# Causal attention and a gated product on one core: Strassen's seven block products for half of the first two batches' first two matrices

## The chip, the cores and the metric

The kernel runs on one core of one Trainium2 chip. The metric is device time in microseconds of one execution, as the median of timed runs; smaller is better. The engines are TensorE (PE, with its weight loads shown apart as PEld), VectorE (DVE), ScalarE (ACT), GpSimd (POOL) and SyncE (SP), whose queue issues every transfer of this kernel.

## The reference, cut to what matters

Causal attention over 4 batches, 12 heads, 448 positions and a head size of 64; its output, put together as 1792 tokens of 768 features, goes through a gated product with d_ff = 1536. The weights arrive as 64-bit floats, everything else as 32-bit floats.

```python
scores = np.where(mask, -1e9, q @ k.T / 8)
attn = exp(scores - max) / (sum + 1e-9)
x = (attn @ v)                      # (1792, 768), heads side by side
out = ((x @ w_a) * (x @ w_b)) @ w_out
```

## The kernel before, in words

**Numbers.** TensorE is fed with 32-bit values split into a rounded part and a rest (x_hi and x_lo, w_hi and w_lo, g_hi and g_lo). A product of one 128x128 weight tile with 448 columns is three matmuls: hi by hi, hi by lo, lo by hi (products, L631 to L639). They are called products below. A 64-bit weight unit of 128x768 is made into 32-bit floats by five DVE instructions and one ACT instruction (convert_unit, L323 to L352), written back to memory as w_keep, and split (split, L360) by one ACT copy and one DVE subtraction.

**Stages.** First comes the attention of batches 0 and 1, by pairs of heads, twelve pairs. Then stage one, the gated product of batches 0 and 1: for each of 12 slices f of d_ff a unit of w_a and one of w_b, and 12 units of w_out, six after f = 5 and six after f = 11. Each of these 36 units is 36 products: 2 batches by 6 slices of 128 rows of the weights, times 3. The attention of batches 2 and 3 runs beside stage one, twelve pairs more; its result goes to memory (x_keep). Then stage two, the gated product of batches 2 and 3, which goes by Strassen throughout: (w_a, w_b) by (batch 2, batch 3) is a 2x2 block product over the lower and upper half of the features, so seven block products of 9 matmuls, 63 in all, stand for the 72 of two units (seven, L712). Its sums of x blocks are made at the end of stage one (take_first, take_second, L590 to L613) from x_keep, and the sums of weight blocks by prepare_all (L681).

**Attention per pair.** PE computes scores into banks; DVE adds the mask and takes the maximum (L448, seven instructions); ACT takes the exponential and the row sum (L454, seven), then divides (L467, seven, in batches 2 and 3); PE transposes (L490), ACT copies the transposed pieces (pt), PE multiplies by v (L529).

**Order.** Nothing is issued as written. Each step is recorded with an engine, a cost and what it reads and writes (Plan.op), and Plan.order lays them out by a list schedule; the index in which steps are recorded sets their priority. uses (L863) records stage one and two and yields after each three products of stage one; attend (L912) records a pair's steps at fixed yields, a new pair every AT[1] = 30 yields, that is two and a half units. convert_next is two units ahead and split_next one unit ahead of the products that use them.

Of the kernel before, what the change touches and what calls it, by code (L numbers as in the profile page):

```python
# [9 lines left out]
F32 = mybir.dt.float32  # L10
# [35 lines left out]
LEAD = (2, 1)  # L46
# [184 lines left out]
def causal_attention_then_gated_product(  # L231
# [15 lines left out]
    def sb(tag, n, shape, dt=F32):  # L247
        return plan.ring(tag, n, lambda i: sbuf.tile(shape, dt, tag=f"{tag}{i}", name=f"{tag}{i}"))
# [71 lines left out]
    def load_kept(u):  # L320
        w_32.append(load_32(u))

    def convert_unit():  # L323
# [17 lines left out]
        plan.op("act", 840, lambda: nc.scalar.activation(  # L341
            e.t, e.t, AF.Copy, bias=-896.0 * 2**23, scale=8.0), [e], [e])
        plan.op("dve", 900, lambda: nc.vector.scalar_tensor_tensor(  # L343
            out=r(), in0=m.t, scalar=2.0**32, in1=low(), op0=ALU.mult, op1=ALU.add), [m, t], [m])
        plan.op("dve", 900, lambda: nc.vector.scalar_tensor_tensor(  # L345
            out=e.t, in0=high(), scalar=0x80000000, in1=e.t,
            op0=ALU.bitwise_and, op1=ALU.bitwise_or), [t, e], [e])
        plan.op("dve", 900, lambda: nc.vector.scalar_tensor_tensor(
            out=wt.t, in0=r(), scalar=2.0**-52, in1=e.t.bitcast(F32),
            op0=ALU.mult, op1=ALU.mult), [m, e], [wt])  # L350
        load(P * UW * 4, lambda: w_keep[u], lambda: wt.t, [wt], [("keep", u)])
        w_32.append(wt)  # L352

    def half():
        h = plan.ring("w", 6, None)
# [221 lines left out]

    raw_x, spare = {}, []

    def both(o, a, b, op, reads, writes):  # L580
        two_input("dve", S, o, a, b, op, reads, writes)

# [26 lines left out]
    for r in range(2):  # L609
        for h in range(2):  # L610
            for f in range(h * HF, (h + 1) * HF):
                order += [("a", f), ("b", f)] if r == 0 else [("s", f)]
            if r == 1:  # L613
                order += [("oo", NP // 2 * h + j) for j in range(NP // 2)]
            else:
                order += [("o", 2 * e + h) for e in range(ET)]
    place = {"a": lambda n: 2 * n, "b": lambda n: 2 * n + 1, "o": lambda n: NA + n}
    in_turn = [place[kind](n) if kind in place else None for kind, n in order]
    xs, a_sb = {}, {}

    def x_parts():
# [16 lines left out]

        plan.op("pe", 3 * 200, mm, [(w, 0), (w, 1), *keys], [ps])  # L639

    to_load = iter(in_turn[:NU])

    def load_next():
        u = next(to_load, None)
        if u is not None:
            load_words(u)

    turned, parted = [0], [0]

    def convert_next():  # L650
        n = turned[0]
        turned[0] += 1
        if n < NU:
            plan.soonest = HOLD[0] + HOLD[1] * n if n <= LEAD[0] else 0.0
            convert_unit()
            plan.soonest = 0.0
            load_next()
        elif n < len(order):
            kind, f = order[n]
            if n == NU:  # L660
                units = []
                for h in range(2):
                    units += [(place["a"](i), place["b"](i), False) for i in range(h * HF, (h + 1) * HF)]
                    units += [(place["o"](4 * j + h), place["o"](4 * j + 2 + h), True) for j in range(NP // 2)]
                weights.extend([load_32(u) for u in units[0][:2]])
                to_prepare[0] = prepare_all(units)

    def split_next():
        n = parted[0]
        parted[0] += 1  # L670
        if n < len(order):
            kind, f = order[n]
            if kind not in ("s", "oo"):
                split_unit()
            elif kind == "s" and f == 0:
# [5 lines left out]
    def prepare_all(units):  # L681

        for n, (_, _, late) in enumerate(units):
            a, b = weights.pop(0), weights.pop(0)
            for i in range(7):
                if i in (0, 4):
                    if n + 1 < len(units):
                        weights.append(load_32(units[n + 1][i // 4]))
                if i == 0:
# [22 lines left out]
    def seven(f, n):  # L712

        bank_a, bank_b, bank_c = (bank("m", 3) for _ in range(3))

# [7 lines left out]
                   (bank_c, "T1", True), (bank_b, "T4", False), (bank_c, "B22", False))  # L723
        for i, (ps, name, first) in enumerate(plan_of):
            next(to_prepare[0], None)
            w = ready.pop(0)
            for k in range(3):
                (hi, hi_key), (lo, lo_key) = (part[k] for part in block[name])
# [2 lines left out]
                s1 = mid()  # L731
                copy("act", S, lambda: s1.t, lambda: bank_a.t[:, :S], [bank_a], [s1], True)
            elif i == 1:
                u2 = sb("acc", 2, [P, S])
                added(u2, bank_b, s1)
            elif i == 2:
                c11 = mid()
                copy("act", S, lambda: c11.t, lambda: bank_a.t[:, :S], [bank_a], [c11], True)
            elif i == 3:
                u3 = sb("acc", 2, [P, S])  # L740
                added(u3, bank_b, s1)
            elif i == 4:
                c22 = mid()
# [6 lines left out]
            else:  # L750
                c12 = mid()
                added(c12, bank_c, u2)
                if f % HF < 3:
# [108 lines left out]

    def uses():  # L863

        for n, (kind, f) in enumerate(order):
            first = n // NU * 2
            convert_next()
            if n == NU - 5:
                make_rooms()
                take_first(0)  # L870
            elif n == NU - 4:
                take_first(1)
            elif n == NU - 3:
                more_rooms()
                take_second(0)
                take_first(2)
            elif n == NU - 2:
                take_second(1)
            elif n == NU - 1:
                take_second(2)  # L880
            if kind == "s":
                if order[n + 1][0] != "o":
                    split_next()
                seven(f, n)
                yield
                continue
            if kind == "oo":
# [153 lines left out]
```

## Time and profile before

| | us |
|---|---|
| median of three timed runs | 636.47 (635.89 to 636.66) |
| the profiled execution's own time | 637.46 |
| its span | 635.4 |
| PE busy | 625.8 (98%) |
| PEld busy | 555.5 (87%) |
| DVE busy | 511.6 (81%) |
| ACT busy | 367.4 (58%) |
| POOL busy | 46.9 (7%) |

The first products stand at 61.5 us, stage two begins at 403.9 us. TensorE's granted clock is full speed (1.00, the 2.4 GHz level) in every slice. A row of the windows view gives, for one stretch, each engine's busy time with the number of its instructions, then the granted clock, the share of the 16 transfer engines and GB/s. A row of the timeline is start, length, engine, line, operation, output and inputs; the length of a DVE or ACT instruction covers a tail that overlaps the next one, so that the cost of one in a dense run is the distance of two starts.

### The profile page before, as it was taken

How to read it: one execution, taken by the hardware profiler on the slowest of the kernel's cores; microseconds unless marked ns; L12 is line 12 of the kernel's file. 1: busy time of each engine (PE TensorE's matmuls, PEld its weight loads, DVE VectorE, ACT ScalarE, POOL GpSimd, SP SyncE). 2: the span in 40 equal slices, each digit the busy share in tenths (PEclk: the TensorE clock that was granted, in tenths of full speed). 3: DMA queues.
4: the chain of work that ended last, by engine and by line, in shares of the span. 5: the costliest groups of instructions: out<-in, count | busy, mean ns of one | idle time of the engine just before them, and what ended most of it. 6: DMA issues, size and time to landing. Idle time of an engine off the chain costs nothing.

```text
span 635.4 us, 11232 instructions
## 1 busy us (share of the span) xinstructions
PE 625.8 (98%) x4034; PEld 555.5 (87%) x4034; DVE 511.6 (81%) x1143; ACT 367.4 (58%) x874; POOL 46.9 (7%) x104
## 2 busy tenths in 40 slices
PE   9999999999999999999999999999999999999997
PEld 6666779899899899899889888999999999999986
DVE  6789988989777576598597597588899768889994
ACT  6989548578478468568567553244555444445430
POOL 3756320000000000000000000000000000000000
PEclk9999999999999999999999999999999999999999
DMA  8636535755828646435542266321212632222622
GB/s 277 222 117 207 171 141 195 246 175 203 296 93 273 221 179 228 169 127 181 183 153 78 90 202 202 108 75 50 76 51 68 194 113 58 67 58 87 219 97 88
DMA packets 41719, 95.89 MB, mean 151 GB/s; under 512 B 4800, under 2 KB 27840, under 8 KB 41664
## 3 DMA queue, kind: packets, MB, share of 16 engines
q1 hardware_dynamic: 41664, 95.18, 45.0%
q8 instruction: 32, 0.52, 0.3%
q14 instruction: 23, 0.19, 0.1%
HBM read 67.24 MB, written 27.92 MB: 150 GB/s over the span
## 4 chain that ended last, share of the span: by engine, by line
PE 87%; DVE 8%; DMA 2%; ACT 1%; issue 0%; POOL 0%; SPq 0%; POOLq 0%; DVEq 0%
PE m L634 61%; PE t L634 7%; PE t L490 5%; PE s L634 3%; PE s L439 3%; PE pv L634 2%; PE t L439 2%; PE pv L510 1%; PE pv L529 1%; PE m L529 1%; DVE early L448 1%; DVE p L448 1%; DVE pt L293 1%; ACT early L454 1%; DVE x_lo L301 1%; DMA acc<-o_keep 1%
## 5 line engine op out<-in xcount | busy, mean ns | idle before, releaser
L634 PE MATMUL m<-x_hi,w_hi 128*128 128x448 f32 x432 | 160.5, 372 | 0.0
L634 PE MATMUL m<-x_hi,w_lo 128*128 128x448 f32 x432 | 156.4, 362 | 0.0
L634 PE MATMUL m<-x_lo,w_hi 128*128 128x448 f32 x432 | 156.1, 361 | 0.0
L634 PEld LDWEIGHTS m<-x_hi,w_lo 128*128 128x128 f32 x432 | 81.0, 188 | 6.2
L634 PEld LDWEIGHTS m<-x_hi,w_hi 128*128 128x128 f32 x432 | 81.2, 188 | 5.4 <-issue 0.2
L634 PEld LDWEIGHTS m<-x_lo,w_hi 128*128 128x128 f32 x432 | 81.1, 188 | 4.7
L454 ACT ACTIVATE p<-p,st 128x448 f32<-128x448 f32 (+6 forms) x126 | 62.5, 498 | 32.6 <-DVE st L448 32.1
L301 DVE TENSOR_TENSOR w_lo<-w,w_hi 128x384 fp32r<-128x384 f32 (+1 forms) x90 | 64.6, 719 | 13.1 <-ACT w_hi L285 12.8
L285 ACT ACTIVATE w_hi<-w 128x384 fp32r<-128x384 f32 (+1 forms) x90 | 58.2, 648 | 27.4 <-PE m L634 12.5
L285 ACT ACTIVATE w_hi<-w_e_s 128x384 fp32r<-128x384 f32 x72 | 37.3, 522 | 52.4 <-PE m L634 30.1
L285 ACT ACTIVATE mid<-m 128x448 f32<-128x448 f32 x60 | 32.6, 544 | 52.3 <-PE m L634 52.2
L634 PE MATMUL m<-g_hi,w_hi 128*128 128x448 f32 x144 | 53.4, 371 | 1.3 <-DVE mid L301 1.2
L634 PE MATMUL m<-g_hi,w_lo 128*128 128x448 f32 x144 | 52.1, 362 | 0.0
L634 PE MATMUL m<-g_lo,w_hi 128*128 128x448 f32 x144 | 52.1, 362 | 0.0
L301 DVE TENSOR_TENSOR w_lo<-w_e_s,w_hi 128x384 fp32r<-128x384 f32 x72 | 39.7, 552 | 11.4 <-ACT w_hi L285 10.3
L285 ACT ACTIVATE pt<-t 128x512 f32<-128x512 f32 x72 | 40.7, 593 | 9.4 <-PE t L490 9.3
L301 DVE TENSOR_TENSOR mid<-m,mid 128x448 f32<-128x448 f32 x36 | 22.4, 621 | 27.1 <-PE m L634 20.2
L345 DVE SCALAR_TENSOR_TENSOR w_e<-w,w_e 128x768 uint32<-128x768 uint32 x36 | 34.5, 961 | 7.5 <-ACT w_e L341 7.4
L285 ACT ACTIVATE g_hi<-mid 128x448 fp32r<-128x448 f32 x42 | 24.2, 575 | 24.7 <-DVE mid L301 24.6
L341 ACT ACTIVATE w_e<-w_e 128x768 uint32<-128x768 uint32 x36 | 30.2, 845 | 13.3 <-DVE w_e L336 12.9
L467 ACT ACTIVATE p<-p,st 128x64 f32<-128x64 f32 (+6 forms) x84 | 34.9, 497 | 1.0 <-DVE st L463 1.0
L343 DVE SCALAR_TENSOR_TENSOR w_m<-w_m,w 128x768 f32<-128x768 uint32 x36 | 34.4, 954 | 0.4
(153 smaller groups left out, 1305.4 us busy)
## 6 DMA issues: line engine op xcount, KB each, us to landing
w<-w SPq DMA_DIRECT2D x36, 768.0 KB, 4.6
w_keep<-w SPq DMA_DIRECT2D x36, 384.0 KB, 3.3
w<-w_keep SPq DMA_DIRECT2D x36, 384.0 KB, 3.1
raw<-qT SPq DMA_DIRECT2D x24, 224.0 KB, 3.9
raw<-kT SPq DMA_DIRECT2D x24, 224.0 KB, 4.2
o_keep<-mid SPq DMA_DIRECT2D x24, 224.0 KB, 2.0
v<-v SPq DMA_DIRECT2D x24, 192.0 KB, 3.3
x_keep<-acc SPq DMA_DIRECT2D x12, 224.0 KB, 2.1
```

The lines of the kernel that those rows point to most:

```text
L285: return nc.scalar.activation(o(), i(), AF.Copy)
L301: plan.op(engine, ns, lambda: e.tensor_tensor(out=o(), in0=a(), in1=b(), op=op), reads, writes)
L341: plan.op("act", 840, lambda: nc.scalar.activation(e.t, e.t, AF.Copy, bias=-896.0 * 2**23, scale=8.0), [e], [e])
L343: plan.op("dve", 900, lambda: nc.vector.scalar_tensor_tensor(out=r(), in0=m.t, scalar=2.0**32, in1=low(), op0=ALU.mult, op1=ALU.add), [m, ...
L345: plan.op("dve", 900, lambda: nc.vector.scalar_tensor_tensor(out=e.t, in0=high(), scalar=0x80000000, in1=e.t, op0=ALU.bitwise_and, op1=ALU ...
L439: x = nc.tensor.matmul(at[r][0].t[to * D:(to + 1) * D, at[r][1]], q[:, r * D:(r + 1) * D], k[:, 0:D * (r + 1)], start=True, stop=True)
L448: return nc.vector.tensor_tensor_reduce(out=view(r), in0=at[r][0].t[:, at[r][1]], in1=mask[:, S - n:], scale=-0.125, scalar=3.0e38, op0=AL ...
L454: return nc.scalar.activation(view(r), view(r), AF.Exp, bias=st.t[:, nm, r:r + 1], scale=-1.0, accum_out=st.t[:, sm, r:r + 1],)
L467: return nc.scalar.activation(view(r), view(r), AF.Copy, scale=st.t[:, rc, r:r + 1])
L490: x = nc.tensor.matmul(t.t[:, P * i:P * (i + 1)], p.t[:, at:at + P], swapped if r in CROSSED else ident, is_transpose=True, start=True, st ...
L529: r = nc.tensor.matmul((ps, more)[row].t[j * D:(j + 1) * D, D * k:S], vt.t[rows, c, j, :], parts[n].t[rows, j, o:o + NR - k, :].rearrange( ...
L634: r = nc.tensor.matmul(ps.t[:, :S], a[:, i, :], x(), start=first and n == 0, stop=last and n == 2, skip_group_check=part)
```

## The change

In stage one the slices f = 6 to 11 of w_a and w_b (the second half of d_ff) go by the seven block products too, with batches 0 and 1 as the two columns of blocks. Units f = 0 to 5 and all units of w_out stay as they were. For this:

- the twelve weight units of f = 6 to 11 are converted earlier, beside the units 3 to 14 (EXTRA), go to memory, and are read back as 32-bit floats when prepare_all makes their sums and splits;
- the sums of x blocks of batches 0 and 1 are made by the new function take, at units 15 to 17 (TAKES), in rooms that other tiles leave (first_rooms);
- the attention of batches 2 and 3 starts a pair every 12 yields, one unit, where it was 30;
- the costs that the planner assumes for a conversion are lowered (840 to 735, 900 to 869).

```diff
+F0 = 6
-AT = (2, 30)
+AT = (2, 12)
+EXTRA = (0, 0, 0, 1, 1, 1, 1, 1, 1, 1, 1, 1, 1, 1, 1)
+TAKES = (15, 16, 17)
...
+    def first_rooms():
+        (x_hi, x_lo), (y_hi, y_lo) = xs[0], xs[1]
+        for name, hi, lo, at in (("B11", x_hi, x_lo, 0), ("B21", x_hi, x_lo, 3), ("T1", y_hi, y_lo, 0), ("B22", y_hi, y_lo, 3)):
+            block[name] = [[((lambda x=x, k=at + k: x.t[:, k, :]), (x, at + k)) for k in range(3)] for x in (hi, lo)]
...
+    def take(k):
+        rooms = [sb("pt", 3, [P, 1024]) for _ in range(2)]
+        b11, b12, b21, b22 = (((lambda t=t, i=i: t.t[:, i * S:(i + 1) * S]), (t, i)) for t in rooms for i in range(2))
+        for (o, key), b, kk in ((b11, 0, k), (b12, 1, k), (b22, 1, k + 3), (b21, 0, k + 3)):
+            hi, lo = xs[b]
+            both(o, lambda hi=hi, kk=kk: hi.t[:, kk, :].bitcast(F32), lambda lo=lo, kk=kk: lo.t[:, kk, :].bitcast(F32), ALU.add,
+                 [(hi, kk), (lo, kk)], [key])
...
+        less(b11, b12, b11)
+        split_block("T1", k, *b11)
+        less(b12, b22, b12)
+        split_block("T3", k, *b12)
+        less(b22, b22, b11)
+        split_block("T2", k, *b22)
+        less(b21, b21, b22)
+        split_block("T4", k, *b21)
...
-                order += [("a", f), ("b", f)] if r == 0 else [("s", f)]
+                order += [("a", f, r), ("b", f, r)] if r == 0 and f < F0 else [("s", f, r)]
...
+    besides = [place[kind](f) for f in range(F0, FT) for kind in "ab"]
...
+    def convert_one(besides=False):
+        convert_unit(besides)
+        load_next()
...
                     if n + 1 < len(units):
                         weights.append(load_32(units[n + 1][i // 4]))
+                    elif r == 0:
+                        convert_one()
                 if i == 0:
-                    s12, s34 = (plan.ring("w_e", 2, lambda j: sbuf.tile([P, UW], F32, tag=f"w_e{j}", name=f"w_e_s{j}"))
+                    tag, count, width = (("pt", 3, 1024), ("w_e", 2, UW))[r]
+                    s12, s34 = (plan.ring(tag, count, lambda j: sbuf.tile([P, width], F32, tag=f"{tag}{j}", name=f"{tag}_s{j}"))
...
+                if r == 0:
+                    both(lambda: c12.t, lambda: c12.t, lambda: c22.t, ALU.mult, [c22], [c12])
+                    part_g(3, f, lambda: c12.t, c12)
+                elif f % HF < 3:
...
+            if n in TAKES:
+                if n == TAKES[0]:
+                    first_rooms()
+                take(TAKES.index(n))
...
             split_next()
+            for _ in range(EXTRA[n] if n < len(EXTRA) else 0):
+                convert_one(True)
```

**On PE, the products of f = 6** (m is a bank, x_hi, x_lo the parts of one batch's x, t a bank of transposes, raw_x a block sum kept where q and k lay). Before, with a pair's transposes between the products:

```order
L490 MATMUL t_2945<-swapped,p_70 128x128
L490 MATMUL t_2945<-ident,p_70 128x128
L490 MATMUL t_2945<-swapped,p_70 128x128 x2
L490 MATMUL t_2953<-ident,p_70 128x128
L490 MATMUL t_2953<-swapped,p_70 128x128
L490 MATMUL t_2953<-ident,p_70 128x128 x2
L634 MATMUL m_2830<-x_hi_431,w_hi 128x448
L634 MATMUL m_2830<-x_lo_450,w_hi 128x448
L634 MATMUL m_2830<-x_hi_431,w_lo 128x448
L634 MATMUL m_2967<-x_hi_944,w_hi 128x448
L634 MATMUL m_2967<-x_lo_966,w_hi 128x448
L634 MATMUL m_2967<-x_hi_944,w_lo 128x448
```

After, in the first f that goes by seven block products:

```order
L677 MATMUL m_3565<-raw_x_3369,w_hi 128x448 x2
L677 MATMUL m_3565<-raw_x_3369,w_lo 128x448
L677 MATMUL m_3565<-raw_x_3435,w_hi 128x448 x2
L677 MATMUL m_3565<-raw_x_3435,w_lo 128x448
L677 MATMUL m_3565<-raw_x_3501,w_hi 128x448 x2
L677 MATMUL m_3565<-raw_x_3501,w_lo 128x448
L677 MATMUL m_3618<-x_hi_944,w_hi 128x448
L677 MATMUL m_3618<-x_lo_966,w_hi 128x448
L677 MATMUL m_3618<-x_hi_944,w_lo 128x448
```

The attention's transposes have moved ahead of this place, and the block sum T3 takes the place of a batch's x. Over the whole program PE has 2376 products where it had 2430; every other kind of matmul keeps its count.

**On DVE, between two pairs of the attention of batches 2 and 3** (w_e, w_m and w are the words, the mantissa and the result of a conversion, w_lo the rest of a split). Before:

```order
L301 TENSOR_TENSOR mid_2253<-m_2219,mid_2071 128x448
L301 TENSOR_TENSOR w_lo<-w_1980,w_hi 128x768
L301 TENSOR_TENSOR g_lo<-mid_2253,g_hi 128x448
L348 SCALAR_TENSOR_TENSOR w_2277<-w_m,w_e_2077 128x768
L301 TENSOR_TENSOR w_lo<-w_2063,w_hi 128x768
L301 TENSOR_TENSOR mid_2300<-m_2204,mid_2137 128x448
L348 SCALAR_TENSOR_TENSOR w_2306<-w_m,w_e_2123 128x768
L301 TENSOR_TENSOR g_lo<-mid_2300,g_hi 128x448
L336 TENSOR_SCALAR w_e_2317<-w_2069 128x768
```

After:

```order
L341 TENSOR_SCALAR w_m<-w_1846 128x768
L348 SCALAR_TENSOR_TENSOR w_e_2002<-w_1846,w_e_2002 128x768
L346 SCALAR_TENSOR_TENSOR w_m<-w_m,w_1846 128x768
L465 TENSOR_SCALAR st<-st 128x7
L304 TENSOR_TENSOR acc_2082<-m_2040,acc_2082 128x384
L467 RECIPROCAL st<-st 128x7
L351 SCALAR_TENSOR_TENSOR w_2102<-w_m,w_e_2002 128x768
L339 TENSOR_SCALAR w_e_2111<-w_1924 128x768
L341 TENSOR_SCALAR w_m<-w_1924 128x768
L304 TENSOR_TENSOR w_lo<-w_2016,w_hi 128x768
L346 SCALAR_TENSOR_TENSOR w_m<-w_m,w_1924 128x768
```

Two conversions and one split now stand between two pairs, and a pair follows every unit. The split of a unit stands 12 to 39 products ahead of the unit's first product, from unit 3 to unit 17; before it stood 0 to 72 ahead there.

**On SP, the end of stage one** (x_keep holds the attention of batches 2 and 3, raw takes it back for the block sums, acc and out belong to w_out). Before:

```order
L304 DMA raw_4274<-x_keep_5_122 128x448
L304 DMA x_keep_5_128<-acc_4276 128x448
L304 DMA w_4297<-w_keep_82 128x768
L304 DMA acc_4312<-o_keep_2_131 128x448
L304 DMA raw_4274<-x_keep_5_128 128x448
L304 DMA w_4338<-w_keep_83 128x768
```

After:

```order
L307 DMA raw_4477<-x_keep_5_128 128x448
L307 DMA raw_4477<-x_keep_5_122 128x448
L307 DMA w_keep_116<-w_4472 128x768
L307 DMA raw_4492<-x_keep_2_119 128x448
L307 DMA raw_4492<-x_keep_2_125 128x448
L307 DMA w_4500<-w_keep_82 128x768
```

The last store to x_keep stood three rows ahead of the load that reads it back; now it stands 51 rows ahead of that load, beside the w_out units that follow f = 5.

## Rows read from the trace of the kernel before

**Rows 1.** The page's first part: busy time and share of each engine.
```profile
PE 625.8 (98%) x4034; PEld 555.5 (87%) x4034; DVE 511.6 (81%) x1143; ACT 367.4 (58%) x874; POOL 46.9 (7%) x104
```

**Rows 2.** Windows: stage one from 96 us, and its last 52 us.
```profile
96.00:403.85 307.85, 306.54 (x2058) 277.41 (x2057) 234.35 (x482) 196.94 (x456) 0.00 (x0) 1.00 0.54 184
352.00:403.85 51.85, 50.54 (x305) 44.86 (x305) 35.28 (x71) 23.52 (x50) 0.00 (x0) 1.00 0.54 168
```

**Rows 3.** Waits of PE, 94 to 600 us: us in total, times, longest.
```profile
PE m L634 <- DVE mid L301: 1.2, 2, 0.9
```

**Rows 4.** The chain that ended last, one pair to the next: start, us, what.
```profile
283.61 0.90 PE t L439 x12
...
286.90 6.21 PE m L634 x30
293.11 0.87 PE t L490 x8
293.98 1.81 PE m L634 x9
295.79 0.87 PE t L490 x8
296.67 12.01 PE m L634 x60
308.67 0.90 PE t L439 x12
```

**Rows 5.** Timeline of DVE in dense runs: start, length, what.
```profile
93.69 0.61 DVE L448 CUSTOM_DVE_ANT_0 p<-s,mask 128x448 f32<-128x448 f32 x1
...
96.09 0.95 DVE L348 SCALAR_TENSOR_TENSOR w<-w_m,w_e 128x768 f32<-128x768 f32 x1
96.96 0.55 DVE L336 TENSOR_SCALAR w_e<-w 128x768 uint32<-128x768 uint32 x1
97.43 0.55 DVE L338 TENSOR_SCALAR w_m<-w 128x768 uint32<-128x768 uint32 x1
...
471.33 0.62 DVE L301 TENSOR_TENSOR v_x<-raw,v_x 128x448 fp32r<-128x448 f32 x1
471.87 0.62 DVE L301 TENSOR_TENSOR raw_x<-raw,raw_x 128x448 fp32r<-128x448 f32 x1
...
475.42 0.55 DVE L301 TENSOR_TENSOR w_e_s<-w,w 128x384 f32<-128x384 f32 x1
475.89 0.55 DVE L301 TENSOR_TENSOR w_e_s<-w_e_s,w 128x384 f32<-128x384 f32 x1
```

**Rows 6.** Timeline of ACT beside one pair: start, length, what.
```profile
122.35 0.67 ACT L454 ACTIVATE p<-p,st 128x448 f32<-128x448 f32 x1 [2.25 <-DVE st L448]
...
125.81 0.53 ACT L285 ACTIVATE acc<-pv 128x448 f32<-128x448 f32 x1
...
127.49 2.90 ACT L467 ACTIVATE p<-p,st 128x64 f32<-128x64 f32 x7
130.29 0.33 ACT L454 ACTIVATE p<-p,st 128x64 f32<-128x64 f32 x1
...
134.14 0.84 ACT L285 ACTIVATE w_hi<-w 128x768 fp32r<-128x768 f32 x1
134.87 1.08 ACT L285 ACTIVATE pt<-t 128x512 f32<-128x512 f32 x2
135.82 0.56 ACT L285 ACTIVATE mid<-m 128x448 f32<-128x448 f32 x1
136.25 1.61 ACT L341 ACTIVATE w_e<-w_e 128x768 uint32<-128x768 uint32 x2
```

**Rows 7.** Windows where DVE, ACT or the transfers are dense.
```profile
48.00:64.00 16.00, 14.90 (x152) 10.50 (x149) 15.20 (x54) 14.56 (x49) 10.40 (x20) 1.00 0.65 205
...
128.00:144.00 16.00, 16.00 (x106) 14.52 (x108) 13.94 (x20) 12.10 (x24) 0.00 (x0) 1.00 0.54 191
...
160.00:176.00 16.00, 16.00 (x120) 14.30 (x119) 11.16 (x28) 8.11 (x22) 0.00 (x0) 1.00 0.83 284
...
440.00:500.00 60.00, 60.00 (x302) 56.25 (x301) 56.43 (x111) 31.01 (x63) 0.00 (x0) 1.00 0.25 78
580.00:600.00 20.00, 20.00 (x102) 18.75 (x101) 19.62 (x39) 11.21 (x22) 0.00 (x0) 1.00 0.65 216
```

More of the change, by code (lines that the diff above doesn't have):

```diff
@@ L321, in load_kept, with convert_unit @@
         w_32.append(load_32(u))
-    def convert_unit():
+    def convert_unit(besides=False):
         u, t = w_64.pop(0)
@@ L340, in convert_unit @@
             op0=ALU.bitwise_and, op1=ALU.bitwise_or), [t], [m])
[L341 removed]
+        plan.op("act", 735, lambda: nc.scalar.activation(
             e.t, e.t, AF.Copy, bias=-896.0 * 2**23, scale=8.0), [e], [e])
[L343 removed]
+        plan.op("dve", 869, lambda: nc.vector.scalar_tensor_tensor(
             out=r(), in0=m.t, scalar=2.0**32, in1=low(), op0=ALU.mult, op1=ALU.add), [m, t], [m])
[L345 removed]
+        plan.op("dve", 869, lambda: nc.vector.scalar_tensor_tensor(
             out=e.t, in0=high(), scalar=0x80000000, in1=e.t,
             op0=ALU.bitwise_and, op1=ALU.bitwise_or), [t, e], [e])
[L348 removed]
+        plan.op("dve", 869, lambda: nc.vector.scalar_tensor_tensor(
             out=wt.t, in0=r(), scalar=2.0**-52, in1=e.t.bitcast(F32),
@@ L351, in convert_unit @@
         load(P * UW * 4, lambda: w_keep[u], lambda: wt.t, [wt], [("keep", u)])
-        w_32.append(wt)
+        if not besides:
+            w_32.append(wt)
     def half():
@@ L578, in causal_attention_then_gated_product, with less @@
     raw_x, spare = {}, []
+    def first_rooms():
+        (x_hi, x_lo), (y_hi, y_lo) = xs[0], xs[1]
+        for name, hi, lo, at in (("B11", x_hi, x_lo, 0), ("B21", x_hi, x_lo, 3), ("T1", y_hi, y_lo, 0), ("B22", y_hi, y_lo, 3)):
+            block[name] = [[((lambda x=x, k=at + k: x.t[:, k, :]), (x, at + k)) for k in range(3)] for x in (hi, lo)]
+        one, two = (places("p", NPB, 4, PW) for _ in range(2))
+        raw = [places("raw", 4, 2, 2 * S) for _ in range(4)]
+        more = [places("v", NVB, 1, 512)[0] for _ in range(2)]
+        block["T2"] = [one[0:3], two[0:3]]
+        block["T3"] = [[x[i] for x in raw[:3]] for i in range(2)]
+        block["T4"] = [[one[3], two[3], raw[3][0]], [raw[3][1], *more]]
+    def take(k):
[5 more added lines that the diff above has]
+                 [(hi, kk), (lo, kk)], [key])
+        def less(o, x, y):
+            both(o[0], x[0], y[0], ALU.subtract, [z[1] for z in (x, y) if z is not o], [o[1]])
+        less(b11, b12, b11)
[6 more added lines that the diff above has]
+        split_block("T4", k, *b21)
     def both(o, a, b, op, reads, writes):
@@ L611, in causal_attention_then_gated_product @@
             for f in range(h * HF, (h + 1) * HF):
-                order += [("a", f), ("b", f)] if r == 0 else [("s", f)]
+                order += [("a", f, r), ("b", f, r)] if r == 0 and f < F0 else [("s", f, r)]
             if r == 1:
-                order += [("oo", NP // 2 * h + j) for j in range(NP // 2)]
+                order += [("oo", NP // 2 * h + j, r) for j in range(NP // 2)]
             else:
-                order += [("o", 2 * e + h) for e in range(ET)]
+                order += [("o", 2 * e + h, r) for e in range(ET)]
+    N0 = [r for _, _, r in order].index(1)
     place = {"a": lambda n: 2 * n, "b": lambda n: 2 * n + 1, "o": lambda n: NA + n}
-    in_turn = [place[kind](n) if kind in place else None for kind, n in order]
+    fast = order.index(("s", F0, 0))
+    besides = [place[kind](f) for f in range(F0, FT) for kind in "ab"]
+    to_load = [place[kind](f) if kind in place else None for kind, f, _ in order[:N0]]
+    for n in reversed(range(len(EXTRA))):
+        some, besides = besides[len(besides) - EXTRA[n]:], besides[:len(besides) - EXTRA[n]]
+        to_load[n + LEAD[0] + 1:n + LEAD[0] + 1] = some
+    assert not besides
+    to_load = iter([u for u in to_load if u is not None])
     xs, a_sb = {}, {}
@@ L652, in convert_next @@
         turned[0] += 1
[L653 to L663, printed above, removed]
+        if n >= len(order):
+            return
+        kind, f, r = order[n]
+        if kind in place:
+            if not (n - 2 < fast + FT - F0 <= n):
+                plan.soonest = HOLD[0] + HOLD[1] * n if n <= LEAD[0] else 0.0
+                convert_one()
+                plan.soonest = 0.0
+        elif n in (fast, N0):
+            units = []
+            for h in range(2):
+                units += [(place["a"](i), place["b"](i), False) for i in range(h * HF, (h + 1) * HF) if r or i >= F0]
+                if r:
                     units += [(place["o"](4 * j + h), place["o"](4 * j + 2 + h), True) for j in range(NP // 2)]
-                weights.extend([load_32(u) for u in units[0][:2]])
-                to_prepare[0] = prepare_all(units)
+            weights.extend([load_32(u) for u in units[0][:2]])
+            to_prepare[0] = prepare_all(units, r)
     def split_next():
@@ L671, in split_next @@
         if n < len(order):
-            kind, f = order[n]
-            if kind not in ("s", "oo"):
+            kind, f, r = order[n]
+            if kind in place:
                 split_unit()
-            elif kind == "s" and f == 0:
+            elif n in (fast, N0):
                 for _ in range(AHEAD):
@@ L679, in causal_attention_then_gated_product, with prepare_all @@
     weights, to_prepare, ready = [], [None], []
-    def prepare_all(units):
+    def prepare_all(units, r):
         for n, (_, _, late) in enumerate(units):
@@ L710, in prepare_all, with seven @@
                 yield
-    def seven(f, n):
+    def seven(f, n, r):
         bank_a, bank_b, bank_c = (bank("m", 3) for _ in range(3))
@@ L725, in seven @@
             next(to_prepare[0], None)
+            if order[n + 1][0] == "o" and i == 4:
+                split_next()
             w = ready.pop(0)
@@ L733, in seven @@
             elif i == 1:
-                u2 = sb("acc", 2, [P, S])
+                u2 = sb("acc", 3 - r, [P, S])
                 added(u2, bank_b, s1)
@@ L739, in seven @@
             elif i == 3:
-                u3 = sb("acc", 2, [P, S])
+                u3 = sb("acc", 3 - r, [P, S])
                 added(u3, bank_b, s1)
@@ L863, in uses @@
     def uses():
-        for n, (kind, f) in enumerate(order):
-            first = n // NU * 2
+        for n, (kind, f, r) in enumerate(order):
+            first = 2 * r
             convert_next()
-            if n == NU - 5:
+            if n in TAKES:
+                if n == TAKES[0]:
+                    first_rooms()
+                take(TAKES.index(n))
+            if n == N0 - 5:
                 make_rooms()
                 take_first(0)
-            elif n == NU - 4:
+            elif n == N0 - 4:
                 take_first(1)
-            elif n == NU - 3:
+            elif n == N0 - 3:
                 more_rooms()
@@ L876, in uses @@
                 take_first(2)
-            elif n == NU - 2:
+            elif n == N0 - 2:
                 take_second(1)
-            elif n == NU - 1:
+            elif n == N0 - 1:
                 take_second(2)
@@ L883, in uses @@
                     split_next()
-                seven(f, n)
+                seven(f, n, r)
                 yield
```

3 lines of the change are left out of this document (1 added, 2 removed).

## The prediction

> **What bounds the kernel now.** I read the page's first part, then the windows of stage one, then who PE waited for, then the chain of waits. PE is busy for 98% of the span, DVE for 81%, ACT for 58% [rows 1]. A busy PE need not be a full PE, so the windows decide: from 96 us to the start of stage two PE is busy for 306.54 of 307.85 us, and the 1.31 us that are missing all lie in the last 52 us [rows 2]. They end with DVE writing a product out of its bank [rows 3]. The chain shows what PE does in between: 60 products in a row take 12.01 us, 0.200 us each, with no gap, and transposes follow products without one [rows 4]. So PE sets the time here, and a product that is not issued gives back 0.200 us, as long as no other engine is late. DVE has 234 us of work in those 308 us, ACT 197 [rows 2]; about 73 us of DVE's time are free, and that is what this change spends.
>
> **Removed: 54 products.** Six slices f go from 72 to 63 products each, 6 x 9 = 54, and the order has 2376 for 2430. At 0.200 us [rows 4] that is 10.8 us of PE, all of it on the path. The Trainium skill's page TensorE: Matmul & The Clock Gate, section Back-to-back issue gap, gives a lone gap of N/2.4 + 2.5 ns, 189 ns for 448 columns; the trace shows 200. By the page the saving would be 10.2 us. The measured distance decides.
>
> **Added on DVE.** Costs are distances of starts in dense runs [rows 5]: 0.54 us for 448 columns (471.33 to 471.87), 0.47 for 384, 0.87 for a three-operand step of 768 and 0.47 for a two-operand one (96.09, 96.96, 97.43); a split of 768, also with two tensor inputs, is put at the 0.87 too. The block sums of x (take) are 3 times 12 instructions of 448, 36 x 0.54 = 19.4 us. Strassen's sums of results add 30 of 448, 16.2 us. The sums of weight blocks are 24 of 384, 11.3 us. The splits become 42 of 384 in place of 12 of 768, 19.7 - 10.4 = 9.3 us. Sum 56 us. Stage one from 96 us then holds 234.35 + 56 = 290 us of DVE in 307.85 - 10.8 = 297 us, 98%. The busy time counts the tail of every instruction that stood alone (0.62 long at 0.54 distance); the 474 instructions of the stretch laid at their distances come to about 227 us, and the demand to 283 us, 95%. Between these two lies the question of this case. ACT gets 12 x 0.47 us of block sums and 42 half copies (some 0.41 each, an estimate from the 0.73 of a whole one [rows 6]) for 12 whole ones, some 14 us on 197, and stays near 71%.
>
> **Moved: the attention of batches 2 and 3.** A pair used to come every 2.5 units and now comes with every unit, beside two conversions where there was one. Per unit:
> PE has 36 x 0.2 = 7.2 us and one pair. The chain gives a pair's price: from 283.61 to 308.67 are 25.06 us with 99 products (30, 9 and 60), 19.8 us, which leaves 5.2 [rows 4]. Sum 12.4 us.
> DVE has seven maxima, 2.40 us (93.69 to 96.09), one sum of 384 and two small steps, 3.1 in all; two conversions at 2 x 0.47 + 3 x 0.87 = 3.55, so 7.1; a split, 0.87; and half of a w_b unit's two multiplications and two rests, 1.1. Sum 12.1 us, 98% of PE's [rows 5].
> ACT has exponentials 3.5 (122.35 to 125.81), divisions 2.8 (127.49 to 130.29), four transposed pieces at 0.48, a result 0.43, so 8.6; two conversion steps at 0.74 and a split 0.73; two copies 0.9. Sum 11.7 us, 94% [rows 6].
> So for twelve units, 12 x 12.4 = 149 us, three engines run within 6% of each other. What PE waits for there no row of before shows as it stands; I bound it. Upper end: in 48 to 64 us, where DVE is busy for 95% and ACT for 91%, PE is idle for 1.1 of 16 us, 6.9% [rows 7]; on 149 us that is 10.3 us. Lower end: 0, since in 440 to 500 us DVE is busy for 94% and in 580 to 600 for 98% while PE has no gap at all [rows 7]; a gain is excluded there since PE had no gap in this stretch before. I take 1.5 us, 1%: these two rows are nearer in kind, because products with weights split ahead fill PE there as here (12 to 39 products ahead by the order), and at 48 us hardly any products were there to fill with.
>
> **Units 15 to 17.** The block sums (19.4 us), a conversion (3.55), two splits (1.7) and the first four weight halves with two sums (six of 384, 2.8) are 27.5 us of DVE against 3 x 7.2 = 21.6 of PE. The 5.9 us too many cost nothing as long as DVE is ahead: the last rest of T4 stands beside the first products of f = 6, whose sixth block needs it 45 products, 9 us, later. If the attention leaves DVE behind, they come on top; the range holds that.
>
> **Transfers.** A dense unit moves a pair in (448 KB of q and k, 224 of v), its result out (224), two units in (1536) and two out (768): 3200 KB in 12.4 us, 264 GB/s. In 160 to 176 us the queue moved 284 GB/s with PE at 16.00 of 16 [rows 7], so I cost it at nothing; the cover is that three units can be loaded ahead of their conversion. The 12 added reads of 384 KB fall behind the attention, where the queue is emptier. SP issues them in order, behind the stores of w_out, and DVE's weight sums would wait for them.
>
> **Recovered.** The 1.31 us of PE's idle time stood at the end of stage one [rows 2], where the attention's last pairs, the block sums of batches 2 and 3 and the last conversions met. Now the attention is over before that, and the last store to x_keep stands 51 rows ahead of its load where it stood 3. I take 1.0, with 0 and 1.3 as ends, because DVE stays full there. Late next is DVE itself. The front up to 96 us and stage two are ordered as before and keep their time.
>
> **Sum.** -10.8 - 1.0 + 1.5 = -10.3 us. Against the profiled execution, 637.46 us with a span of 635.4, that is 627.2 and 625.1; the median of the runs is 1.0 us below the profiled one, so 636.47 - 10.3 = 626.2 us.
>
> **Rivals.**
> **DVE binds stage one.** DVE waits, too, for ACT and PE, and 95% by distances may be more than it can hold over 297 us. In 440 to 500 us it held 56.43 of 60, by distances 55.8, 93% [rows 7]. At 93%, 283 us of work take 304, 7 us more than PE's 297, in place of the 1.5: 632. For it: nothing dense of before lasted more than 60 us. Against it: in those 60 us PE set the pace and DVE was idle because it had nothing to do. The Trainium skill's Perfetto Trace Analysis, section Identifying the Most-Contended Engine, says that matmul busy time does not tell how close TensorE is to its limit, that the weight loads' share does, and that for VectorE occupancy is a fair measure. By that rule DVE at 95 to 98% passes the weight loads, 277.41 of 307.85 us, 90% [rows 2], and becomes the bound, the 632 of this rival. The trace does not bear the first half out: weight loads stand at 56.25 of 60 us while PE has no gap [rows 7].
> **The gain is eaten.** If the dense twelve units lose the whole 10.3 us of the row at 48 us and nothing is recovered, 636.47 - 10.8 + 10.3 = 636.0.
> **Slower than before.** A conversion goes DVE, ACT, DVE, and so does each pair's maximum, exponential and reciprocal. DVE works in order, so with two conversions and a pair in each unit it stands at the head of its queue waiting for ACT, itself at 94%, and behind it stand the reads out of PE's three banks; PE then waits for a bank. Price: in 128 to 144 us DVE was busy for 13.94 of 16 us, 87%, beside ACT at 76% [rows 7]; at 87% its 283 us take 325, 28 more than 297, so 636.47 - 10.8 + 28 = 654. It decides from the point where DVE's share falls below 283/308 = 92%. Against it: PE did not wait in that row, the conversions were early.
> That fewer products are not issued at all is no rival: the order shows them gone.
>
> **How the numbers follow.** Forecast, 623.8 to 629.5: 0.70. DVE binds, 629.5 to 635.2: 0.16. Eaten, 635.2 to 637.7: 0.06. Slower, above 637.7: 0.08. The low end takes no new wait, 1.3 recovered and 0.6 for the spread of the runs (635.89 to 636.66). For 8 in 10 the range reaches into the second case past its 632, to 633; above lie some 0.04 of it and the last two cases. 0.2% is 1.3 us, about what a measurement can tell from no change: faster 0.86, same 0.06, slower 0.08.
>
> **What would show it.** Right: PE without gaps from 96 us to stage two, which begins near 393.6 us; seven block products at 63 x 0.2 = 12.6 us for each f; DVE's busy share of stage one above 93%; the wait of PE for DVE below 3 us. The second case shows as many gaps of PE of 0.3 to 1 us that end with DVE, between 100 and 260 us or ahead of f = 6. Slower shows as DVE idle behind ACT (w_e, exponentials) in the same stretch with PE waiting for banks. A longer front or a stage two with gaps would say that I overlooked something outside stage one.

## The result, and the profile after

The changed kernel takes 627.18 us (median of four runs, 626.25 to 627.53) beside 636.19 (635.89 to 636.66) for the kernel before in the same series: a ratio of 0.9855, interval 0.9838 to 0.9873, or -9.0 us. In a later series it took 627.49 beside 635.85, ratio 0.9872 (0.9851 to 0.9893). The forecast was 626.2, within 623.8 to 633.0. The sign and the mechanism were right; the saving came out 1.3 us smaller than -10.3, and the experiments find where that went.

The profiled execution has 627.53 us and a span of 625.7. Line 634 of before is line 677 of after (679 where a DVE step is added below), 301 is 304, 285 is 288, 448 is 452, 490 is 494. The page's first part, beside [rows 1]:

```profile
PE 616.0 (98%) x3980; PEld 543.7 (87%) x3980; DVE 564.3 (90%) x1263; ACT 383.5 (61%) x916; POOL 47.1 (8%) x104
```

PE issues 54 matmuls fewer and is busy for 9.8 us less; DVE has 52.7 us more work, for 56 predicted. PE's timeline where stage two begins (start, length, what):

```profile
394.20 0.36 PE L677 MATMUL m<-g_hi,w_lo 128*128 128x448 f32 x1
394.40 0.36 PE L677 MATMUL m<-x_hi,w_hi 128*128 128x448 f32 x1
```

The first x_hi product behind the g products opens stage two, at 394.40; before it stood at 403.85, and 393.6 was predicted. Windows of after: stage one from 96 us, as in [rows 2]; the twelve dense units; the place where the attention's last pair meets the block sums; and the first slices that go by seven block products:

```profile
96.00:394.40 298.40, 296.62 (x2001) 265.58 (x2000) 286.22 (x598) 212.92 (x495) 0.00 (x0) 1.00 0.62 203
...
120.00:240.00 120.00, 120.00 (x1035) 104.70 (x1034) 117.62 (x286) 113.73 (x293) 0.00 (x0) 1.00 0.77 252
...
230.00:254.00 24.00, 22.77 (x178) 19.60 (x177) 23.97 (x43) 19.04 (x40) 0.00 (x0) 1.00 0.92 307
...
272.00:312.00 40.00, 39.65 (x196) 36.01 (x195) 38.43 (x75) 20.21 (x40) 0.00 (x0) 1.00 0.39 121
```

DVE works for 286.22 of 298.40 us, 96%, inside the 95 to 98% of the prediction. In the dense units DVE stands at 98% and ACT at 95%, and PE still has no gap in 120 us. The idle time of PE lies behind them, from 252 us on. PE's waits, 94 to 600 us, for [rows 3] (us in total, times, longest):

```profile
PE m L677 <- DVE acc L304: 1.6, 2, 1.2
PE t L677 <- ACT mid L288: 0.6, 1, 0.6
PE m L677 <- DVE g_lo L304: 0.2, 1, 0.2
```

The second line lies in stage two. The longest wait, in PE's and DVE's timelines (in brackets the idle time and what ended it):

```profile
252.03 0.47 PE L677 MATMUL m<-g_hi,w_hi 128*128 128x448 f32 x1 [1.24 <-DVE acc L304]
```

```profile
247.71 0.95 DVE L346 SCALAR_TENSOR_TENSOR w_m<-w_m,w 128x768 f32<-128x768 uint32 x1
248.58 0.95 DVE L348 SCALAR_TENSOR_TENSOR w_e<-w,w_e 128x768 uint32<-128x768 uint32 x1
249.45 0.62 DVE L304 TENSOR_TENSOR pt<-x_hi,x_lo 128x448 f32<-128x448 f32 x1
249.99 0.95 DVE L351 SCALAR_TENSOR_TENSOR w<-w_m,w_e 128x768 f32<-128x768 f32 x1
250.85 0.62 DVE L304 TENSOR_TENSOR pt<-x_hi,x_lo 128x448 f32<-128x448 f32 x1
251.42 0.56 DVE L304 TENSOR_TENSOR acc<-m,acc 128x384 f32<-128x384 f32 x1
```

The sum into acc at 251.42 frees the bank m that PE's next product wants. Ahead of it in DVE's order stand two conversions and the first block sums (pt<-x_hi,x_lo), back to back. So DVE was late there by a little over a microsecond.

### The profile page after: what moved, and what is told of

It reads as the page before. It is cut to its first block, busy times and chain, and to the rows that moved or that the text cites. A ratio compares the mean times of both kernels' runs of the same rounds, so it can differ in the third digit from the quotient of the medians.

```text
span 625.7 us, 11349 instructions
## 1 busy us (share of the span) xinstructions
PE 616.0 (98%) x3980; PEld 543.7 (87%) x3980; DVE 564.3 (90%) x1263; ACT 383.5 (61%) x916; POOL 47.1 (8%) x104
## 4 chain that ended last, share of the span: by engine, by line
PE 82%; DVE 13%; ACT 2%; DMA 1%; issue 1%; POOL 0%; SPq 0%; POOLq 0%; DVEq 0%
PE m L677 56%; PE t L677 7%; PE t L494 5%; PE s L677 3%; PE s L443 3%; PE pv L677 2%; PE t L443 2%; PE pv L533 2%; PE pv L514 2%; DVE p L452 2%; DVE w_lo L304 1%; PE m L533 1%; DVE early L452 1%; DVE pt L296 1%; ACT early L458 1%; DMA raw<-x_keep 1%
## 5 line engine op out<-in xcount | busy, mean ns | idle before, releaser
L677 PE MATMUL m<-x_hi,w_hi 128*128 128x448 f32 x360 | 135.2, 376 | 0.0
L677 PE MATMUL m<-x_lo,w_hi 128*128 128x448 f32 x360 | 130.5, 363 | 0.0
L677 PE MATMUL m<-x_hi,w_lo 128*128 128x448 f32 x360 | 130.2, 362 | 0.0
L677 PEld LDWEIGHTS m<-x_hi,w_hi 128*128 128x128 f32 x360 | 67.8, 188 | 5.5 <-issue 0.5
L677 PEld LDWEIGHTS m<-x_hi,w_lo 128*128 128x128 f32 x360 | 67.5, 187 | 4.9
L677 PEld LDWEIGHTS m<-x_lo,w_hi 128*128 128x128 f32 x360 | 67.7, 188 | 3.4
L458 ACT ACTIVATE p<-p,st 128x128 f32<-128x128 f32 (+6 forms) x126 | 62.3, 498 | 8.2 <-DVE st L452 8.1
L304 DVE TENSOR_TENSOR w_lo<-w,w_hi 128x384 fp32r<-128x384 f32 (+1 forms) x96 | 63.0, 656 | 0.2 <-ACT w_hi L288 0.2
L677 PE MATMUL m<-p_x,w_hi 128*128 128x448 f32 x144 | 43.5, 363 | 0.0
L304 DVE TENSOR_TENSOR mid<-m,acc 128x448 f32<-128x448 f32 x48 | 29.7, 619 | 8.3 <-PE m L677 7.5
```

What stands on the lines that cost most here:

```text
L304: plan.op(engine, ns, lambda: e.tensor_tensor(out=o(), in0=a(), in1=b(), op=op), reads, writes)
L458: return nc.scalar.activation(view(r), view(r), AF.Exp, bias=st.t[:, nm, r:r + 1], scale=-1.0, accum_out=st.t[:, sm, r:r + 1],)
L677: r = nc.tensor.matmul(ps.t[:, :S], a[:, i, :], x(), start=first and n == 0, stop=last and n == 2, skip_group_check=part)
```

## Experiments

**1. The attention's place alone.** The kernel before, with the denser attention and nothing else:

```diff
-AT = (2, 30)
+AT = (2, 12)
```

> The kernel before with the attention of batches 2 and 3 alone made dense (a pair every 12 yields in place of 30), no block products in stage one. PE binds: the same 2430 products and the same pairs, so 636 us, less at most the 1.3 us of idle time at the end of stage one: 635 to 637. Rival, the attention's place is what gained the 9 us: 627 to 629.

Measured: 636.31 us, ratio 1.0008 (0.9999 to 1.0017), as expected. Its profile has no wait of PE left between 94 and 600 us, where before had 1.2 [rows 3], and yet the median did not move. So the idle time that the prediction meant to recover is no gain in the median. The gain is there in the traces: from the first product to stage two are 342.35 us before (61.50 to 403.85) and 341.28 here (61.42 to 402.70). Nor is that idle time what lifts the profiled execution of before, 637.46 us, 1.3 us above its median: the profile of experiment 2 has the same wait and stands at 636.50. Why the 1.1 us don't reach the median stays open.

**2. The planner's costs alone.** The kernel before, with

```diff
-        plan.op("act", 840, lambda: nc.scalar.activation(
+        plan.op("act", 735, lambda: nc.scalar.activation(
-        plan.op("dve", 900, lambda: nc.vector.scalar_tensor_tensor(
+        plan.op("dve", 869, lambda: nc.vector.scalar_tensor_tensor(
...
```

> The kernel before with the lower assumed costs of a conversion alone (735 and 869). PE binds: 635.5 to 636.7, no change. Rival, the better plan is part of the gain: 633 to 635.

Measured: 636.05 us, ratio 1.0001 (0.9992 to 1.0011), and the same wait of 1.2 us for mid as before. Neither of the two moves is worth anything by itself. Together with experiment 1 this leaves the removed products as the source of the gain; the sum further below counts them in the traces. One thing holds for every experiment here: the planner lays out all steps anew after each edit, so a difference holds the new order of the steps too.

**3. How much room has DVE?** The changed kernel, with one or four more DVE maxima of 448 columns in each of the twelve pairs that run in stage one, 6.4 and 25.7 us of DVE in all (the range is 4 in the second kernel):

```diff
+        for _ in range(1):
+            two_input("dve", S, lambda: t.t, lambda: t.t, lambda: t.t, ALU.max, [], [t])
```

> The changed kernel with one more DVE instruction of 448 columns in each of the twelve pairs of batches 2 and 3 (a maximum of the result with itself, which leaves it as it is): 12 x 0.54 = 6.4 us of DVE in the attention stretch. If DVE still had room there (12.1 of 12.4 us a unit), the most is absorbed: 628 to 631. Rival, DVE sets the time of the stretch already: the whole 6.4 us come on top, 633.6.

> The same with four such instructions in each pair, 25.7 us of DVE. A unit then asks 14.2 us of DVE against 12.4 of PE: DVE binds, and all but the room that was left shows: 644 to 650. If DVE had room of 10 us or more in stage one (the low reading of the demand, 95%), no more than 643.

Measured: 629.04 us (ratio 0.9892, 0.9876 to 0.9909), +1.9 for 6.4 us; and 650.53 us (1.0228, 1.0213 to 1.0243), +23.4 for 25.7, just above the 644 to 650 expected. So DVE hid 4.5 us of the first addition. With four more, PE's two largest groups of waits (us in total, times, longest), the window around the longest, the four microseconds behind it, and PE at a shorter one:

```profile
PE m L679 <- DVE mid L304: 5.7, 2, 5.3
PE m L679 <- DVE w_lo L304: 4.8, 3, 3.0
```

```profile
200.00:216.00 16.00, 10.75 (x52) 9.61 (x48) 14.78 (x34) 12.13 (x32) 0.00 (x0) 0.79 0.48 167
205.00:209.00 4.00, 3.54 (x12) 3.06 (x13) 4.00 (x12) 3.23 (x7) 0.00 (x0) 0.50 0.62 232
```

```profile
296.89 0.47 PE L679 MATMUL m<-x_hi,w_hi 128*128 128x448 f32 x1 [0.63 <-ACT mid L288]
...
298.95 0.47 PE L679 MATMUL m<-x_hi,w_lo 128*128 128x448 f32 x1 [1.39 <-DVE w_lo L304]
...
300.86 0.58 PE L679 MATMUL m<-p_x,w_lo 128*128 128x448 f32 x1
301.23 0.95 PE L679 MATMUL m<-p_x,w_hi 128*128 128x448 f32 x2
```

DVE had become the bound, and TensorE's granted clock, 0.79 in the first window and 0.50 (the 1.2 GHz level) in the second, fell with the waits. Behind three of them (5.25, 3.03 and 1.39 us) products stood 0.37 us apart in place of 0.20. By the distances of starts that cost some 5.7 us, so that of the 23.4 about 17.7 are DVE's lateness and DVE hid some 8 of 25.7 us (estimates from these rows). Its room in stage one is thus no single figure: 6.4 us more already cost 1.9, while of 25.7 a third stayed hidden. This is the first rival's mechanism, and it begins a few microseconds of DVE away from the changed kernel.

**4. Is PE still the bound?** The changed kernel without the block product T4 in each f of stage one, 54 products fewer again; what T4 feeds is missing from the output:

```diff
-                products(ps, w, k, hi, lo, first and k == 0, k == 2, [hi_key, lo_key], True)
+                if r or name not in ("T4",):
+                    products(ps, w, k, hi, lo, first and k == 0, k == 2, [hi_key, lo_key], True)
```

> The changed kernel with 54 products more left out: the block product with T4 in each of the six f of stage one (its result is left out of the sums, all work of DVE and ACT stays). If PE still binds stage one, 54 x 0.200 = 10.8 us less: 616.4. Rival, DVE, busy for 96% of the stage, binds once PE has 10.8 us less: 621 to 625, with PE waiting for DVE.

Measured: 620.39 us, ratio 0.9763 (0.9747 to 0.9778): -6.8 of the 10.8 us. Waits of PE and the window of the slices by seven block products:

```profile
PE m L677 <- DVE w_lo L304: 3.0, 2, 2.3
PE m L677 <- DVE acc L304: 1.2, 1, 1.2
```

```profile
300.00:388.00 88.00, 84.90 (x421) 78.03 (x420) 86.32 (x154) 41.86 (x75) 0.00 (x0) 1.00 0.50 166
```

The time lies between the two forecasts, 616.4 and 621 to 625, and both theories hold in part. Most of a product is still paid by PE, and DVE, now at 98% of this window (95% in the changed kernel), takes the rest. The next 54 products are worth less than two thirds of their 10.8 us.

**5. DVE's block sums on POOL.** The twelve sums hi + lo of take go to POOL, which has nothing to do in stage one:

```diff
-            both(o, ..., ALU.add,
+            two_input("pool", S, o, ..., ALU.add,
```

> The changed kernel with the twelve sums of x_hi and x_lo at units 15 to 17 on POOL in place of DVE, 6.5 us of DVE less where it was full. If PE's waits there (1.24, 0.34 us) come from DVE's backlog, they go: 625.4 to 626.3. Rival, POOL is slower than DVE (and shares the memory with it), so the sums come late or DVE's steps grow: 627.5 to 630.

Measured: 638.48 us, ratio 1.0040 (1.0026 to 1.0054): +11.3, slower than the kernel before and far above both forecasts. DVE's timeline while POOL works on its sums (the first stands from 252.69 for 2.28 us, the next three from 254.94, 4.48 us together, two more from 260.57 for 2.79):

```profile
255.00 1.56 DVE L304 TENSOR_TENSOR pt<-pt,pt 128x448 f32<-128x448 f32 x1 [0.56 <-POOL pt L304]
256.49 1.91 DVE L304 TENSOR_TENSOR w_lo<-w,w_hi 128x768 fp32r<-128x768 f32 x1
258.32 1.57 DVE L304 TENSOR_TENSOR raw_x<-pt,raw_x 128x448 fp32r<-128x448 f32 x1
259.82 0.61 DVE L304 TENSOR_TENSOR pt<-pt,pt 128x448 f32<-128x448 f32 x1
260.35 0.55 DVE L339 TENSOR_SCALAR w_e<-w 128x768 uint32<-128x768 uint32 x1
260.82 1.55 DVE L304 TENSOR_TENSOR pt<-pt 128x448 f32<-128x448 f32 x1
```

A two-operand step of DVE takes 0.61 us alone and 1.56 beside POOL, as long as one of POOL's (18.6 us for 12, 1.575 each). So what DVE gave away came back as blocking. The Trainium skill's page SBUF — State Buffer, section SBUF: two separate sides, says that a DVE instruction with two SBUF inputs and a GpSimd instruction that reads SBUF share a port pair, and that whichever starts first has it for the whole instruction; these rows agree. PE then waited (us in total, times, longest):

```profile
PE m L677 <- ACT mid L288: 4.5, 2, 3.9
PE m L677 <- DVE acc L304: 3.9, 2, 2.0
```

That is 8.4 of the 11.3 us. From 256 to 272 us the granted clock was 0.89, and behind the wait of 3.9 us nine products stood 0.37 us apart, near twice their 0.20, 1.5 us more. The same came a second time, behind a wait half as long:

```profile
286.29 0.47 PE L677 MATMUL m<-x_hi,w_hi 128*128 128x448 f32 x1 [0.59 <-ACT mid L288]
...
290.28 0.77 PE L677 MATMUL m<-raw_x,w_hi 128*128 128x448 f32 x2 [1.91 <-DVE acc L304]
```

```profile
290.00:294.00 4.00, 3.72 (x11) 3.31 (x12) 1.46 (x4) 0.52 (x1) 0.00 (x0) 0.59 0.57 197
```

Eleven products, to 294.18 us, take 3.9 us for 2.2. Waits of 8.4 us and products at half speed for 1.5 and 1.7 us more come to 11.6, all of the 11.3.

**6. The attention over later.** A pair every 14 yields in place of 12:

```diff
-AT = (2, 12)
+AT = (2, 14)
```

> The changed kernel with a pair every 14 yields in place of 12, 1.17 units: a pair and its share of conversions ask 12.1 to 13.6 us of DVE in 13.6 us of PE, but the attention ends two units later, beside the block sums at units 15 to 17. If DVE's backlog there makes the waits, they grow: 628 to 632. Rival, the loss lies in the dense attention: 626 to 627.

Measured: 638.47 us, ratio 1.0038 (1.0023 to 1.0053): +11.3, far above both theories. A less dense attention ends later (its last product with v stands at 265.7 us, where it stood at 250.5), and the block sums wait in DVE's order for the rooms that its last pairs hold. DVE's timeline, PE's, and a window:

```profile
266.14 0.63 DVE L304 TENSOR_TENSOR pt<-x_hi,x_lo 128x448 f32<-128x448 f32 x1 [2.96 <-PE pv L533]
```

```profile
285.29 0.74 PE L677 MATMUL m<-x_hi,w_lo 128*128 128x448 f32 x1 [5.08 <-DVE w_lo L304]
...
289.19 0.57 PE L677 MATMUL m<-x_hi,w_hi 128*128 128x448 f32 x1
289.56 0.57 PE L677 MATMUL m<-x_lo,w_hi 128*128 128x448 f32 x1
289.93 0.57 PE L677 MATMUL m<-x_hi,w_lo 128*128 128x448 f32 x1
```

```profile
284.00:290.00 6.00, 4.71 (x13) 4.19 (x14) 4.62 (x11) 2.09 (x4) 0.00 (x0) 0.53 0.32 79
```

The first slice by seven block products waits 5.1 us for a rest w_lo that stands behind all block sums. Then 15 products, to 291.05 us, take 5.8 us for 3.0, some 0.37 each: the granted clock is 0.53 in that window, near the lower of its two levels (1.2 GHz of 2.4), after the engine had stood still for 5 us. That is 2.8 us more. With PE's waits of stage one, 8.2 us in all (5.1 for w_lo, 2.9 for ACT, 0.2), it makes up 11.0 of the 11.3 us. The prediction's third rival decided "from the point where DVE's share falls below 92%"; here DVE has the same 286 us of work in a longer stage one, 92.5%, and the kernel is slower than before. Its end was right, its reason (DVE at the head of its queue behind ACT) was not: it waited for a room.

**7. The conversions earlier.** The changed kernel, with the twelve conversions beside units 1 to 12 in place of 3 to 14, so that none of them stands among the block sums:

```diff
-EXTRA = (0, 0, 0, 1, 1, 1, 1, 1, 1, 1, 1, 1, 1, 1, 1)
+EXTRA = (0, 1, 1, 1, 1, 1, 1, 1, 1, 1, 1, 1, 1, 0, 0)
```

> The changed kernel with the twelve early conversions beside units 1 to 12 in place of 3 to 14, so that none stands beside the attention's last pairs and the block sums. If PE's waits of 1.24 and 0.34 us come from DVE's queue being full from 238 to 284 us, they shrink and the time falls by up to 1.6 us: 625.6 to 626.8. Rival, DVE is full over the whole attention stretch, and the conversions only push the backlog to its start: 627 to 630.

> The changed kernel once more, unaltered, so that it stands beside the next run on the same chip. Expected 626.3 to 627.6 us, ratio to the kernel before 0.985.

> The changed kernel with the twelve conversions beside units 1 to 12 instead of 3 to 14, on the same chip as the changed kernel itself. Theory: the 1.6 us that TensorE waits for VectorE around 252 us come from the conversions of units 13 and 14 running into the block sums, so this is 1.2 to 2.0 us below the changed kernel, 625.2 to 626.0. Rival: the 625.48 measured once was the chip, and the two come out within 0.5 us of each other.

Measured: 625.48 us the first time, ratio to before 0.9835 (0.9821 to 0.9850); then, on one chip, 625.15 (0.9834, 0.9816 to 0.9853) beside 627.49 for the changed kernel. That is -2.3 us, a little more than the 1.2 to 2.0 expected. It beats both kernels. Waits of PE, 94 to 600 us, and windows:

```profile
PE t L677 <- ACT mid L288: 0.6, 1, 0.6
```

```profile
96.00:391.90 295.90, 295.90 (x2002) 265.30 (x2001) 284.48 (x598) 211.11 (x493) 0.00 (x0) 1.00 0.62 205
...
120.00:240.00 120.00, 120.00 (x1034) 104.10 (x1026) 117.31 (x288) 112.13 (x288) 0.00 (x0) 1.00 0.78 253
...
272.00:312.00 40.00, 40.00 (x202) 37.50 (x201) 35.77 (x70) 18.27 (x37) 0.00 (x0) 1.00 0.29 95
```

PE has no gap from 96 us to stage two. In 272 to 312 us it issues 202 matmuls where the changed kernel issued 196 (197 in its second profile): some 1.1 us, of which that row's idle time shows 0.35. So a wait of PE costs more than the profile books as idle. The changed kernel's PE timeline shows it:

```profile
279.25 0.37 PE L677 MATMUL m<-x_hi,w_lo 128*128 128x448 f32 x1
279.95 0.68 PE L677 MATMUL m<-raw_x,w_hi 128*128 128x448 f32 x2 [0.34 <-DVE acc L304]
280.46 0.36 PE L677 MATMUL m<-raw_x,w_lo 128*128 128x448 f32 x1
```

Three products from 279.25 to 280.46 take 1.21 us in place of 0.60; the loss is 0.61, the idle time booked is 0.34.

**8. Did the early order leave room?** The early kernel without T4 in its six f (nine in the expectation is a slip; 54 products are six times nine), and the early kernel with one DVE maximum more in each pair (edits as in 4 and 3).

> The early conversions and block product T4 left out of each of the nine fast f of stage one (54 products of 0.200 us fewer; the part of the output that T4 feeds lacks it). In the late order leaving it out gave 6.8 of 10.8 us, with TensorE waiting for VectorE. Theory A: what was lost there is VectorE's share of the stretch from 300 to 388 us, which the early order doesn't alter: 618.0 to 620.0, 6 to 7.5 us below the early kernel, waits for w_lo near 355 and 365 us. Theory B: it was the backlog that the block sums left, which the early order takes away: 614.7 to 616, the whole 10.8 us, no wait over 1 us.

> The early conversions and one more VectorE operation of 448 columns in each pair of stage one, 6.4 us of VectorE in all. In the late order this cost 1.9 of 6.4 us. Theory A: the room of VectorE belongs to the whole stage, and with the early order 1.6 us more of it is free: 0 to 0.8 us above the early kernel, 625.5 to 626.3. Theory B: the room is set where the block sums run and is no larger: again about 1.9 us, 627.0 to 627.8.

Measured: 619.17 us (617.19 to 620.22, the widest spread here) without T4, ratio 0.9736 (0.9710 to 0.9762), -6.0 of 10.8; theory A. The profiled execution is the fastest of the four, 617.19. Its single wait of stage one, 2.3 us for a w_lo at 362 us, stands where conversions of w_out and the block sums of batches 2 and 3 share DVE. With the maximum, 630.88 us (0.9924, 0.9906 to 0.9943): +5.7 of 6.4, more than in the late order and outside both expectations. From the first product to stage two it takes 5.1 to 5.3 us more than the early kernel in its two profiles, though PE's booked waits there come to 1.6 us. Windows of this kernel, ahead of the dense units and of them:

```profile
96.00:120.00 24.00, 24.00 (x188) 20.57 (x187) 23.36 (x53) 23.20 (x62) 0.00 (x0) 1.00 0.67 220
...
120.00:240.00 120.00, 119.11 (x980) 100.54 (x979) 118.87 (x286) 111.25 (x284) 0.00 (x0) 1.00 0.72 241
```

In the dense units DVE stands at 99% and PE issues 980 matmuls, 54 of all kinds fewer than in the early kernel's row, with 0.9 us booked as idle. In 96 to 120 us DVE is busy for 23.36 of 24 us, as in the early kernel; in the changed one it was 21.51. So the early order won its gain at the block sums and gave up 1.9 us of DVE's room ahead of the dense units. That a lack of lead there makes each pair late is an argument from these rows and wasn't tested. It has a rival that these runs leave open, the order on PE, which the planner made anew. The chain over one pair in the early kernel, then in this one (start, us, what):

```profile
188.74 3.86 PE m L677 x18
...
193.04 1.21 PE m L677 x6
194.25 0.87 PE t L494 x8
```

```profile
188.42 5.61 PE m L679 x27
...
194.46 0.61 PE m L679 x3
...
196.44 1.02 PE t L494 x8
```

Fewer products stand between a pair's pieces, and by the distances of starts the whole 5.1 us lie at the attention's matmuls (81.3 us for 76.2 in the early kernel's profile beside it); from product to product nothing was lost. Theory A's number is wrong in any case: the time freed at the block sums did not pay for the addition.

## Why the prediction was right, point by point

**What bounds.** Right: PE is without a gap wherever DVE is in time, and the removed products pay 0.200 us each (see the sum below). Experiments 1 and 2 rule out the other two moves as a source.

**Added on DVE.** 286.22 us of busy time in stage one, where the two ways of counting gave 283 and 290. ACT stands at 71% there, as said.

**The twelve dense units.** Predicted 149 us and 1.5 us of new waits; units 3 to 14 took 146.1 us, from 105.9 us to 252.03, and the only booked wait is the 1.24 us at their very end. The lower end held for the pairs, although DVE stood at 98% and ACT at 95%.

**Units 15 to 17: the step that failed.** "The 5.9 us too many cost nothing as long as DVE is ahead." DVE was not ahead: the conversions beside units 13 and 14 still stood in its order when the block sums came. That costs the 1.24 us at 252 us and the delays up to 312 us, together about 2.3 us by experiment 7. The prediction had named the condition and put no price on it. That the forecast is only 1 us off is partly luck: the 1.5 us of waits put at the dense units, which ran without a gap, stand in for most of this loss.

**Recovered.** Predicted 1.0. The waits of [rows 3] are gone, but experiment 1 shows that taking them away alone leaves the median where it was. In the median this term was nothing; in the traces it is 1.1 us, as predicted, and the new waits are then 2.6 to 3.1 instead of 1.5 (82.08 to 84.69 and 85.15 in the count below).

**The sum.** Between the first product and stage two, the time that isn't 0.200 us per product was 83.15 us before (342.35 - 1296 x 0.2), 85.15 and 84.69 in two profiles after, 82.08 in experiment 1 and 82.6 in the early kernel. So waits and recovery together came to +1.5 to +2.0 us instead of +0.5. With -10.8 that makes -8.8 to -9.3 us of stage one; the first product 0.65 us earlier, which differs from run to run, and 0.25 us behind stage two make up the span's -9.7. The profiled executions differ by 9.9 us and the medians by 9.0, since the one of before stood 1.3 us above its median and the one of after 0.35.

**Transfers.** Right: at 307 GB/s and a share of 0.92 in the row of 230 to 254 us no wait of PE ended with a transfer. The store to x_keep took 6.3 us to land where it had taken 2.1, and nobody waited for it.

**Rivals.** That DVE binds was not the case here, but nearer than the 0.16 sounded: of 6.4 us more it hid 4.5 (experiment 3). The slower case was real as well; two small changes (5 and 6) lead to 638.5 us.

## What to carry to other kernels

Where one engine sets the pace and another stands at 95%, count the second engine's work stretch by stretch; a surplus of a few microseconds in one place shows up as a wait there, even when the stage as a whole has room. When work has to be added to such an engine, put it where its queue holds nothing that the first engine needs next; moving twelve conversions by two units was worth 2.3 us here. And an idle time in one profile is not yet a gain in the median: experiment 1 took such a 1.2 us away, and the median stayed.

## What was not expected of the hardware

- A POOL sum of 448 columns (1.575 us beside DVE) holds up DVE's two-operand steps on SBUF, 0.61 to 1.56 us, so that idle POOL was no help to a full DVE.
- A wait of TensorE of 3.9 us (experiment 5) and one of 5.1 us (experiment 6) were each followed by 9 and 15 products at about half speed, 0.37 for 0.20 us, the second with a granted clock of 0.53 in its window; the changed kernel, with a longest wait of 1.24 us, kept 1.00. The length of a single wait doesn't settle it: the same followed waits of 1.91 us (experiment 5, nine products after one of 0.59) and 1.39 us (experiment 3, two products after one of 0.63), but not the waits of 2.01 us at 254.50 us (experiment 5) or of 2.29 us (experiments 4 and 8). Where the clock fell, a late engine was paid for twice.
- The idle time that the profile books for PE was a part only of what a wait cost: 0.34 of 0.61 us at 279.95 us in the changed kernel.
